# A planner's prices for VectorE and GpSimd working side by side, ten staging tiles, and two early steps for two batches

## The chip, the cores and the metric

The kernel runs on one core of a Trainium2 chip. The metric is the device time in microseconds (us) of one execution. A profiled execution gives the span from its first to its last instruction, a trace of every instruction on each engine, and the TensorE clock that was granted.

The engines are named as in the profile: PE is TensorE (matrix products), PEld its weight loads, DVE is VectorE, ACT is ScalarE, POOL is GpSimd, SP is SyncE, which issues nearly all DMAs. Each engine executes its own queue strictly in order and waits on semaphores for the others.

## The reference

Chunked attention with a few memory keys, then a gated feed-forward layer whose gate mixes positions:

```python
# q, k, v: 4 batches, 8 heads, 768 positions, 64 wide; mem_k, mem_v: 8 rows
for c in range(24):                       # chunks of 32 queries
    k_full = concat(mem_k, k[c*32-16 : c*32+40]); v_full = likewise
    a = softmax(q_c @ k_full.T / 8)
    out_c = a @ v_full
x = out as (4, 768, 512)
h = relu(x @ w_in)                        # 512 x 1024
u, v = h[..., :512], h[..., 512:]
v_n = (v - mean(v)) / sqrt(var(v) + 1e-6) # over the last axis
v_s = w_spatial @ v_n + b_spatial         # 768 x 768 over positions
y = (u * v_s) @ w_out                     # 512 x 512
```

All arrays are float32.

## The kernel before

**Arithmetic.** The feed-forward and later products split each fp32 operand into a high part (a cast on ScalarE) and a low part (a subtraction of the cast from the original, on VectorE or GpSimd), and use three matmuls: high x high, low x high, high x low. The spatial product and the product with w_out are each done by a scheme of seven half-size products, p1 to p7, in place of eight. Sums and differences of left operands (`total`, L651) and their two parts (`left`, cast L664 and subtraction L667) are made on the fly; those of right operands are made once from w_spatial and w_out (`right_hand`, L881, and `split`, L853 and L857).

**Stages.** (1) 24 attention units, each four chunks of one batch for all heads: scores and the previous unit's weighted values in one burst of matmuls (L395), maximum, subtraction, exponent, sum (`softmax`), a transpose (L475), the scaling of the result (L430), a transpose back (L490) and its split into high and low (L495, L499). (2) The feed-forward products `ffn_v` and `ffn_u` (L528 to L530) are interleaved with attention and run on to the end of that stage. ffn_v's result is normalised in a staging tile and stored to DRAM; ffn_u's is stored directly. (3) For each batch, `spatial(b)`: steps p1, p2, p6, p5, p7, p4, p3. Each step has two output tiles of 128 x 384, nine matmuls each. The results are copied out of PSUM into staging tiles (ACT L731), joined with other banks (DVE L737) and multiplied into u on GpSimd (L745, the gate). (4) For each batch, `ffn_o(b)`: steps p1, p6, p5, p7, p4, p3, p2 on the gated tiles, with copies (L780), joins (L786) and stores.

w_in and w_out arrive as the two 32-bit halves of float64 numbers. `from_f64` unpacks a row block: two ScalarE scalings (L824, L829), two VectorE operations (L833 and L834, called the shift) and a GpSimd addition (L839). w_out can be put in place only when the feed-forward products are done, since its tiles take the memory of w_in.

**Buffers.** `sizes` gives the tiles of each ring. `st` is the staging ring, 8 tiles of 128 x 512: ffn_v results, unpacked weight rows, temporaries of `right_hand` for w_out, and results of (3) and (4) before they are joined or gated. A tile is given again when the use eight allocations back has ended. PSUM rings: `f` has 3 banks, `y` 5. The gated tiles `ug` are 6, the normalised halves `vr` 2.

**The plan.** The kernel first only records operations, each with an engine, a price in us, what it reads and writes, and a rank. `Plan.order` then simulates the engines by these prices: at each turn it takes, over all engines, the operation that can start earliest, and among several of one engine that could start at the same time the one of lowest rank. The order of planned starts is the order of each engine's queue. An operation marked `alone` (the shift, and ffn_v's normalisation) is planned only where GpSimd is free, and GpSimd waits for its planned end. Prices are linear in the width:

```python
    def act(n): return 0.18 + 0.00087 * n
    def dve(n): return 0.17 + 0.00102 * n
    def pool_(n): return 0.15 + 0.0024 * n
```

Neither a VectorE operation nor a GpSimd one is priced differently where the other engine works at the same time.

Ranks: attention unit i has 10 i; ffn products on PE 10000 plus a running number `seq`; unpacking and splitting w_out 260; totals, left operands, copies, joins and gates of (3) and (4) 1000 + `seq`; matmuls of (3) and (4) 10000 + `seq`. `seq` grows in the order in which the steps are defined, so the loop at L1004 sets who comes first: for each batch b it defines the loads, then step p1 of `spatial(b)` (L1012), then `ffn_o(b - 1)`, then the other steps of `spatial(b)`. For b = 3 one step of `ffn_o(2)`, its last, is held back until after the first of `ffn_o(3)`.

Of the kernel before, what the change touches and what calls it, by code (L numbers as in the profile page):

```python
# [25 lines left out]
class Plan:  # L26
# [12 lines left out]

    def op(self, eng, us, fn, r=(), w=(), rank=0.0, mb=0.0, tail=0.0, after=None, alone=False, drag=1.0):  # L40
        n = len(self.ops)
        deps, begun = set(), set()
        if after is not None:
            begun.add(after)
        for key in r:
            deps.add(self.writer.get(key))
            self.readers.setdefault(key, []).append(n)
        for key in w:
            deps.add(self.writer.get(key))
            deps.update(self.readers.get(key, ()))  # L50
            self.writer[key], self.readers[key] = n, []
        deps -= {None, n}
        held = {k[:2] for k in (*r, *w) if isinstance(k, tuple) and k[0] in self.rings}
        for s in held:
            if s not in self.slots and s[0] not in self.loose:
                if s[0] in self.newest:
                    begun.add(self.newest[s[0]])
                self.newest[s[0]] = n
            self.slots.setdefault(s, []).append(n)
        begun -= deps  # L60
        self.ops.append((eng, us, fn, deps, rank, mb, tail, held, begun, alone, drag))
        return n

    def order(self):
# [8 lines left out]
        pipe, landed = self.landing, []  # L73
        lone = 0.0
        taken = {ring: [] for ring in self.rings}
# [6 lines left out]
        while len(out) < len(ops):  # L82
# [20 lines left out]
            (t, _, n), e = best  # L103
            _, us, _, _, _, mb, tail, held, _, alone, drag = ops[n]
            for s in held:
# [4 lines left out]
            if alone:  # L110
                lone = t + us
            if mb:
                pipe = max(pipe, t + us) + mb * drag / self.rate
                end[n] = pipe + self.landing
                landed.append((end[n], mb))
            else:
                end[n] = t + us + tail
# [25 lines left out]
def tile_chunked_attention_gmlp(  # L143
# [43 lines left out]

    sizes = {"f": 3, "sx": 1, "pt": 2, "xt": 1, "y": 5, "st": 8, "big": 4, "uo": 2, "x": 2, "vm": 3,
             "q": 2, "k": 2, "kT": 2, "p": 1, "xs": 1, "pT": 1, "vr": 2, "op": 4, "sm": 2, "ug": 6, "ot": 11}
# [6 lines left out]
    def dve(n):  # L196
        return 0.17 + 0.00102 * n
# [194 lines left out]
    def burst(i, rank, split=False):  # L392
# [19 lines left out]
        for what in (whole if split else [whole]):  # L412
            reads, writes = [], []
            us = 0.4
            if "s" in what:
                reads += qk_keys(i, "q") + [("kmain", i % NK, 0), ("kmain", i % NK, 1), ("kmem", i % NK)]
                writes.append(("sx", i, 0))
                us += 0.6
            if "a" in what:
                reads += [("pT", i - 1)] + v_keys(i - 1)  # L420
                writes.append(("sx", i, 1))
                us += 0.7
            op("PE", us, lambda what=what: go(what), r=reads, w=writes, rank=rank, tail=0.25)
# [11 lines left out]
    def softmax(i, rank):  # L435
# [30 lines left out]
        op("ACT", act(512), exp, w=[("p", i)], rank=rank)  # L466
        op("DVE", dve(512) + 0.36, den, r=[("p", i)], w=[("rec", i)], rank=rank + 0.6)

    def flip(i, rank):
        if i < NU:  # L470
# [6 lines left out]
            def copy():  # L477
                nc.scalar.copy(alloc("pT", i, [P, T, P], F32), t_["pt", i])
            op("PE", 0.45, turn, r=[("p", i)], w=[("pt", i)], rank=rank, tail=0.25)
            op("ACT", act(512) - 0.04, copy, r=[("pt", i)], w=[("pT", i)], rank=rank)  # L480
        if i >= 1:
# [15 lines left out]
            def low():  # L497
                x = t_["x", n]
                nc.vector.tensor_tensor(x[:, 1, :, o:o + UT], t_["xt", j], x[:, 0, :, o:o + UT].bitcast(F32),  # L499
                                        op=ALU.subtract)  # L500
            op("PE", 0.45, turn_x, r=[("xs", j)], w=[("xt", j)], rank=rank - 0.5, tail=0.25)
            op("ACT", act(512) - 0.04, high, r=[("xt", j)], w=[("x", n, tt, "h")], rank=rank - 0.5)
# [46 lines left out]
    def ffn_v(b, tt):  # L549
# [31 lines left out]
        op("ACT", act(512), relu, r=[("f", n)], w=[k_], rank=rank)  # L581
        op("DVE", 1.05, stat, r=[k_], w=[("ve", i)], rank=rank)
        op("POOL", 0.6, power, r=[("ve", i)], w=[("rstd", i)], rank=rank)
# [53 lines left out]
    def product(kind, b, steps, halves, chunks, width, parts, N, right, right_keys, sum_eng, seed, done):  # L637
# [5 lines left out]
        def total(name, in0, in1, o, keys, to=None):  # L643
# [3 lines left out]
            def go():  # L647
# [3 lines left out]
                {"DVE": nc.vector, "POOL": nc.gpsimd}[sum_eng].tensor_tensor(a, in0(), in1(), op=o)  # L651
            op(sum_eng, dve(W) if sum_eng == "DVE" else pool_(W), go, r=keys, w=[sm], rank=rank)
            return (lambda: t_[sm].rearrange("p (s n) -> p s n", s=chunks)), [sm]

        def left(name, of, keys):
# [12 lines left out]
            op("ACT", act(W), high, r=keys, w=[(*ok, "h")], rank=rank)  # L668
            op("DVE", dve(W), low, r=[*keys, (*ok, "h")], w=[(*ok, "l")], rank=rank)
            return half, [(*ok, "h"), (*ok, "l")]  # L670
# [178 lines left out]
    def split(eng, n, dst, of, reads, writes, rank):  # L849
# [8 lines left out]
        op("ACT", act(n), high, r=reads, w=[(*w, "h") for w in writes], rank=rank)  # L858
        op(eng, pool_(n) if eng == "POOL" else dve(n), low, r=[*reads, *[(*w, "h") for w in writes]], w=writes, rank=rank)

# [143 lines left out]
    for b in range(B + 1):  # L1004
        if b < B:
# [5 lines left out]
            spatials.append(spatial(b))  # L1011
            next(spatials[b])  # L1012
        if b:
# [59 lines left out]
```

## Time and profile before

| | us |
|---|---|
| median of 3 runs (lowest, highest) | 395.51 (395.07, 395.77) |
| the profiled execution, its own time | 395.85 |
| its span, first to last instruction | 394.1 |
| PE busy in the span | 368.4 (93%) |
| DVE busy | 281.0 (71%) |
| ACT busy | 210.2 (53%) |
| POOL busy | 157.5 (40%) |

The granted TensorE clock was 1.000 throughout. Shares are averages over stages with different limits. In a timeline row, the columns are the start and the duration in us, the engine, the line of the program, the operation with what it writes and reads, and a count where several are merged; a bracket gives the idle time of that engine directly before the row and the instruction whose end ended it. Waits are read from semaphores, so where one instruction waits for several, the last of them is named. In the chain of waits, a piece's length is the part of it that lies on the chain.

### The profile page before, as it was taken

To read this page: it belongs to the slowest core of one execution; us is meant where nothing else is said; L and a number is where in the kernel's file an instruction comes from. 1 tells how busy PE (TensorE), PEld (TensorE's weight loads), DVE (VectorE), ACT (ScalarE), POOL (GpSimd) and SP (SyncE) were. 2 spreads that over 40 slices of the span, in tenths; PEclk is the share of its full clock that TensorE was granted. 3 is DMA by queue.
4 is the path that set the end of the run, shared out by engine and by line. 5 is a ranking of instruction groups with operands and counts; after the bars stand their busy time and mean duration, and the time that the engine had idled before them with its cause. 6 is when DMAs were issued, how large, how long until landed. Compare 5 with 4: busy or idle time off the path is not lost.

```text
span 394.1 us, 8707 instructions
## 1 busy us (share of the span) xinstructions
PE 368.4 (93%) x3428; PEld 335.0 (85%) x3428; DVE 281.0 (71%) x465; ACT 210.2 (53%) x368; POOL 157.5 (40%) x161
## 2 busy tenths in 40 slices
PE   1659899999999999999999998899999999999996
PEld 1437688898898988988889898799999999999996
DVE  7975965756856558866575499978956794788594
ACT  4765646575456557464434475438434734473361
POOL 8433762193621177601012968770226033403520
PEclk9999999999999999999999999999999999999999
DMA  8998567676575683786603768403640562040014
GB/s 231 309 232 210 129 202 230 183 251 185 182 219 160 235 221 112 211 223 206 187 29 136 257 237 278 136 25 121 210 153 0 162 233 89 0 175 27 2 40 161
DMA packets 47356, 64.93 MB, mean 165 GB/s; under 512 B 4434, under 2 KB 38866, under 8 KB 47316
## 3 DMA queue, kind: packets, MB, share of 16 engines
q1 hardware_dynamic: 46900, 64.25, 53.5%
q8 instruction: 27, 0.44, 0.5%
q10 hardware_dynamic: 416, 0.13, 0.1%
q14 instruction: 13, 0.11, 0.1%
HBM read 45.49 MB, written 18.87 MB: 163 GB/s over the span
## 4 chain that ended last, share of the span: by engine, by line
PE 80%; DVE 8%; issue 2%; ACT 2%; POOL 1%; ACTq 0%
PE y L689 16%; PE f L689 12%; PE f L528 12%; PE sx L395 11%; PE f L530 11%; PE f L529 11%; PE xt L490 3%; PE pt L475 3%; DVE wout L857 2%; DVE sm L651 2%; DVE op L667 2%; POOL ug L745 1%; DVE st L737 1%; ACT op L664 1%; DVE st L834 0%
## 5 line engine op out<-in xcount | busy, mean ns | idle before, releaser
L745 POOL TENSOR_TENSOR ug<-st,ug 128x384 f32<-128x384 f32 x32 | 43.8, 1380 | 79.6 <-DVE st L737 62.0
L528 PE MATMUL f<-x,win_h 128*128 128x384 f32 x128 | 45.8, 358 | 0.0
L574 POOL TENSOR_TENSOR rstd<-ve,mhalf 128x1 f32<-128x1 f32 x24 | 13.5, 562 | 77.4 <-DVE ve L570 75.7
L664 ACT CAST op<-sm 128x768 fp32r<-128x768 f32 x32 | 26.3, 837 | 32.5 <-DVE sm L651 29.9
L530 PE MATMUL f<-x,win_h 128*128 128x384 f32 x128 | 43.2, 338 | 0.0
L529 PE MATMUL f<-x,win_l 128*128 128x384 f32 x128 | 43.0, 336 | 0.0
L528 PE MATMUL f<-win_h,x 128*128 128x512 f32 x96 | 41.6, 433 | 0.0
L689 PE MATMUL y<-wsp,op 128*128 128x384 f32 x192 | 39.5, 341 | 2.0 <-ACT st L731 1.2
L395 PE MATMUL sx<-kmain,q 128*32 128x128 f32 x768 | 28.5, 294 | 11.3 <-ACT kmain L377 9.3
L377 ACT COPY kmain<-k 64x640 f32<-64x640 f32 x48 | 34.7, 724 | 6.8 <-DMA k<-in_k_dram 4.0
L530 PE MATMUL f<-win_l,x 128*128 128x512 f32 x96 | 38.2, 398 | 0.0
L529 PE MATMUL f<-win_h,x 128*128 128x512 f32 x96 | 38.1, 397 | 0.0
L430 DVE TENSOR_TENSOR xs<-sx,rec 128x512 f32<-128x512 f32 x24 | 16.6, 690 | 29.7 <-PE sx L395 29.7
L667 DVE TENSOR_TENSOR op<-sm,op 128x768 fp32r<-128x768 f32 x32 | 33.6, 1056 | 5.3 <-ACT op L664 4.9
L689 PE MATMUL y<-wout,op 128*128 128x256 f32 x288 | 36.2, 280 | 0.8 <-ACT ot L780 0.7
L395 PEld LDWEIGHTS sx<-kmain,q 128*32 128x32 f32 x768 | 21.5, 117 | 18.2 <-POOL vmain L369 10.1
L689 PEld LDWEIGHTS y<-wsp,op 128*128 128x128 f32 x192 | 33.9, 188 | 3.2 <-ACT st L731 1.9
L689 PEld LDWEIGHTS y<-wout,op 128*128 128x128 f32 x288 | 34.9, 188 | 1.2 <-ACT ot L780 0.9
L369 POOL COPY vmain<-memv 8x1024 f32<-8x1024 f32 x22 | 23.8, 1083 | 17.6 <-PE sx L395 16.2
L689 PE MATMUL f<-wsp,op 128*128 128x384 f32 x144 | 29.4, 339 | 1.5 <-DVE op L667 1.5
L599 ACT ACTIVATE uo<-f 128x384 f32<-128x384 f32 x32 | 15.6, 490 | 26.8 <-PE f L530 17.7
L689 PE MATMUL f<-wout,op 128*128 128x256 f32 x216 | 27.3, 280 | 0.0
(100 smaller groups left out, 833.4 us busy)
## 6 DMA issues: line engine op xcount, KB each, us to landing
vmain<-in_v_dram SPq DMA_DIRECT2D x48, 128.0 KB
vn_far<-st SPq DMA_DIRECT2D x24, 256.0 KB
u_far<-uo SPq DMA_DIRECT2D x32, 192.0 KB
vr<-vn_far SPq DMA_DIRECT2D x8, 768.0 KB
ug<-u_far SPq DMA_DIRECT2D x16, 384.0 KB
q<-in_q_dram SPq DMA_DIRECT2D x11, 512.0 KB
out_dram<-ot SPq DMA_DIRECT2D x36, 128.0 KB
vmain<-in_v_dram SPq DMA_DIRECT2D x47, 96.0 KB
```

The lines of the kernel that those rows point to most:

```text
L369: {"DVE": nc.vector, "POOL": nc.gpsimd}[eng].tensor_copy(to, of)
L377: nc.scalar.copy(kmain[i % NK][rows, :, r, :, 0:CH], k_of(i)[rows].rearrange("p t (c s) -> p t c s", s=CH))
L395: nc.tensor.matmul(o, w_, m, start=True, stop=True, skip_group_check=True)
L430: nc.vector.tensor_tensor(xs, t_["sx", i][:, 1], rec.unsqueeze(3).broadcast_to([P, T, 2, D]), op=ALU.mult)
L528: nc.tensor.matmul(o, lh, rh, start=(j == 0), stop=False)
L529: nc.tensor.matmul(o, ll, rh, start=False, stop=False)
L530: nc.tensor.matmul(o, lh, rl, start=False, stop=(j == len(pairs) - 1))
L599: op("ACT", act(HT), lambda: nc.scalar.activation(alloc("uo", i, [P, HT], F32), t_["f", n], AF.Relu), r=[("f", n)], w=[("uo", i)], rank=rank)
L664: nc.scalar.copy(half(0), of())
L667: nc.vector.tensor_tensor(half(1), of(), half(0).bitcast(F32), op=ALU.subtract)
L689: nc.tensor.matmul(o, x, y, start=first and m == 1 and not (seed and bank != "x"), stop=m == 3 * chunks, skip_group_check=True)
L745: nc.gpsimd.tensor_tensor(g, t_[st(x)], g, op=ALU.mult)
```

## The change

1. `op` takes a mark `shared`. In `order`, when a marked VectorE operation is placed at a time when GpSimd's planned work is not over, its price grows by (1 - 1/1.75) of the overlap left, at most by 0.75 of the price. When any GpSimd operation is placed while the last marked VectorE operation is not over, its price grows likewise with 1.4 in place of 1.75. Marked are `den` in `softmax`, the statistics of `ffn_v`, `total`, the subtraction in `left` (L667), and the subtraction in `split` where VectorE does it (L857).
2. Prices: a burst with both scores and values 1.70 to 1.88, one with values alone 1.10 to 1.00; `den` by 0.07 more; a transpose 0.45 to 0.47; the statistics 1.05 to 1.08.
3. The ring `st` has 10 tiles in place of 8.
4. At L1012, batches 1 and 2 define two steps of `spatial(b)` (p1 and p2) ahead of `ffn_o(b - 1)`; batches 0 and 3 one, as before.

```diff
-    def op(self, eng, us, fn, r=(), w=(), rank=0.0, mb=0.0, tail=0.0, after=None, alone=False, drag=1.0):
+    def op(self, eng, us, fn, r=(), w=(), rank=0.0, mb=0.0, tail=0.0, after=None, alone=False, drag=1.0, shared=False):
...
-        lone = 0.0
+        lone = both = 0.0
...
-            _, us, _, _, _, mb, tail, held, _, alone, drag = ops[n]
+            _, us, _, _, _, mb, tail, held, _, alone, drag, shared = ops[n]
+            beside, pace = {"DVE": (free["POOL"] if shared else 0.0, 1.75), "POOL": (both, 1.4)}.get(e, (0.0, 1.0))
+            if beside > t:
+                us += min((beside - t) * (1 - 1 / pace), us * (pace - 1))
...
+            if shared:
+                both = t + us
...
-    sizes = {"f": 3, "sx": 1, "pt": 2, "xt": 1, "y": 5, "st": 8, "big": 4, "uo": 2, "x": 2, "vm": 3,
+    sizes = {"f": 3, "sx": 1, "pt": 2, "xt": 1, "y": 5, "st": 10, "big": 4, "uo": 2, "x": 2, "vm": 3,
...
-                us += 0.7
+                us += 0.88 if "s" in what else 0.6
...
-        op("DVE", dve(512) + 0.36, den, r=[("p", i)], w=[("rec", i)], rank=rank + 0.6)
+        op("DVE", dve(512) + 0.43, den, r=[("p", i)], w=[("rec", i)], rank=rank + 0.6, shared=True)
...
-            op("PE", 0.45, turn, r=[("p", i)], w=[("pt", i)], rank=rank, tail=0.25)
+            op("PE", 0.47, turn, r=[("p", i)], w=[("pt", i)], rank=rank, tail=0.25)
...
-        op("DVE", 1.05, stat, r=[k_], w=[("ve", i)], rank=rank)
+        op("DVE", 1.08, stat, r=[k_], w=[("ve", i)], rank=rank, shared=True)
...
-            op("DVE", dve(W), low, r=[*keys, (*ok, "h")], w=[(*ok, "l")], rank=rank)
+            op("DVE", dve(W), low, r=[*keys, (*ok, "h")], w=[(*ok, "l")], rank=rank, shared=True)
...
-            next(spatials[b])
+            for _ in range((1, 2, 2, 1)[b]):
+                next(spatials[b])
```

`total` and `split` get the mark in the same way as `left`, where their engine is VectorE, and the transpose back gets the price of the transpose.

More of the change, by code (lines that the diff above doesn't have):

```diff
@@ L60, in op @@
         begun -= deps
-        self.ops.append((eng, us, fn, deps, rank, mb, tail, held, begun, alone, drag))
+        self.ops.append((eng, us, fn, deps, rank, mb, tail, held, begun, alone, drag, shared))
         return n
@@ L500, in low @@
                                         op=ALU.subtract)
-            op("PE", 0.45, turn_x, r=[("xs", j)], w=[("xt", j)], rank=rank - 0.5, tail=0.25)
+            op("PE", 0.47, turn_x, r=[("xs", j)], w=[("xt", j)], rank=rank - 0.5, tail=0.25)
             op("ACT", act(512) - 0.04, high, r=[("xt", j)], w=[("x", n, tt, "h")], rank=rank - 0.5)
@@ L651, in go @@
                 {"DVE": nc.vector, "POOL": nc.gpsimd}[sum_eng].tensor_tensor(a, in0(), in1(), op=o)
-            op(sum_eng, dve(W) if sum_eng == "DVE" else pool_(W), go, r=keys, w=[sm], rank=rank)
+            op(sum_eng, dve(W) if sum_eng == "DVE" else pool_(W), go, r=keys, w=[sm], rank=rank,
+               shared=sum_eng == "DVE")
             return (lambda: t_[sm].rearrange("p (s n) -> p s n", s=chunks)), [sm]
@@ L858, in split @@
         op("ACT", act(n), high, r=reads, w=[(*w, "h") for w in writes], rank=rank)
-        op(eng, pool_(n) if eng == "POOL" else dve(n), low, r=[*reads, *[(*w, "h") for w in writes]], w=writes, rank=rank)
+        op(eng, pool_(n) if eng == "POOL" else dve(n), low, r=[*reads, *[(*w, "h") for w in writes]], w=writes, rank=rank,
+           shared=eng == "DVE")
     def w_in_part(c, part, rank, load_rank, sub_eng):
```

## The prediction

> **What bounds the kernel now.** I read three views in this order: busy time by stretch, the timelines of TensorE, ScalarE (ACT), VectorE (DVE) and GpSimd (POOL) where TensorE has gaps, and the chain of waits. The stretches are cut where the work changes: start, attention with the first products, the change-over to the spatial product, the steady middle and the end.
>
> ```profile
> 0.00:60.00 60.00, 41.77 (x472) 31.80 (x473) 45.98 (x81) 35.34 (x60) 32.83 (x42) 1.00 0.82 220
> 60.00:233.60 173.60, 173.60 (x1931) 152.43 (x1930) 112.02 (x227) 95.95 (x163) 65.88 (x76) 1.00 0.63 191
> 233.60:268.30 34.70, 30.60 (x174) 28.86 (x172) 31.38 (x33) 17.90 (x34) 26.15 (x19) 1.00 0.43 147
> 268.30:360.00 91.70, 91.70 (x637) 91.70 (x638) 70.60 (x96) 47.39 (x88) 25.00 (x18) 1.00 0.37 126
> 360.00:394.10 34.10, 30.68 (x221) 30.16 (x219) 21.07 (x31) 13.60 (x27) 7.68 (x7) 1.00 0.17 59
> sum 394.10, PE 368.36 PEld 334.95 DVE 281.04 ACT 210.18 POOL 157.54; mean PE 73.67 PEld 66.99 DVE 56.21 ACT 42.04 POOL 31.51
> ```
>
> Columns are the stretch, its length, then busy us and instructions of PE, PE's weight load, DVE, ACT and POOL. TensorE (PE) does 368.36 us of work that the change neither adds to nor takes from. Its gaps are 60.00 - 41.77 = 18.23 us at the start, none to 233.6, 34.70 - 30.60 = 4.10 at the change-over, none to 360, and 34.10 - 30.68 = 3.42 at the end: 25.75 together. Two stretches that hold 265 of 394 us have no gap at all, so an order of work that is better there for VectorE or GpSimd brings nothing. The change can shorten only the 18.23 and the 4.10; it can lengthen anything. The change-over's gaps, one by one:
>
> ```profile
> 246.07 1.15 PE L689 MATMUL f<-wsp,op 128*128 128x384 f32 x5 [1.47 <-DVE op L667]
> ...
> 250.68 1.14 PE L689 MATMUL y<-wsp,op 128*128 128x384 f32 x5 [0.62 <-DVE op L667]
> ...
> 254.31 1.31 PE L689 MATMUL y<-wsp,op 128*128 128x384 f32 x6 [0.38 <-ACT st L731]
> ...
> 256.99 1.32 PE L689 MATMUL y<-wsp,op 128*128 128x384 f32 x6 [0.84 <-ACT st L731]
> ...
> 268.25 2.37 PE L689 MATMUL y<-wout,op 128*128 128x256 f32 x18 [0.67 <-ACT ot L780]
> ```
>
> The number in brackets is the gap before the row, and what ended it. 1.47 + 0.62 come from a VectorE subtraction (L667, the low half of a left operand), 0.38 + 0.84 from a copy out of PSUM on ScalarE (L731), 0.67 from another such copy (L780). That is 3.98 of the 4.10; the 0.12 left is spread too thin to treat. Each engine runs its queue in the order that the plan wrote, so I look at what stands ahead of those releasers. ScalarE first:
>
> ```profile
> 253.26 0.62 ACT L853 CAST wout<-st 128x512 fp32r<-128x512 f32 x1 [0.75 <-POOL st L881]
> 253.78 0.47 ACT L731 COPY st<-y 128x384 f32<-128x384 f32 x1
> 255.94 0.62 ACT L853 CAST wout<-st 128x512 fp32r<-128x512 f32 x1 [1.68 <-POOL st L881]
> 256.46 0.86 ACT L731 COPY st<-y 128x384 f32<-128x384 f32 x2
> ```
>
> Before both copies (253.78 and 256.46, L731) stands a cast of w_out (L853) that itself waited 0.75 and 1.68 us for GpSimd. The copies' banks were done: ScalarE was held by an instruction that was queued too early. VectorE:
>
> ```profile
> 242.73 1.61 DVE L857 TENSOR_TENSOR wout<-st,wout 128x512 fp32r<-128x512 f32 x1
> 244.26 0.55 DVE L737 TENSOR_TENSOR st<-f,st 128x384 f32<-128x384 f32 x1
> 244.73 1.29 DVE L667 TENSOR_TENSOR op<-sm,op 128x768 fp32r<-128x768 f32 x1
> ...
> 249.68 0.95 DVE L667 TENSOR_TENSOR op<-sm,op 128x768 fp32r<-128x768 f32 x1
> 250.54 2.07 DVE L667 TENSOR_TENSOR op<-vr,op 128x768 fp32r<-128x768 f32 x1
> ...
> 260.98 0.96 DVE L667 TENSOR_TENSOR op<-ug,op 128x768 fp32r<-128x768 f32 x1 [1.78 <-ACT op L664]
> ```
>
> The subtraction that PE waits for at 246.07 (244.73, L667) stands behind a subtraction for w_out (242.73, 1.61) and a join (244.26, L737). No bracket stands in the first five rows: VectorE has work without a break, 31.38 of 34.70 us in this stretch. The last row shows the first pause, 1.78 us, after 258. So two different faults make the change-over's gaps: a queue in the wrong order (ScalarE) and a full engine (VectorE).
>
> **The change, part by part.** No instruction is added or removed. What changes is what the plan believes, and so the order in each queue and the slot that a tile takes.
>
> *VectorE and GpSimd stretch each other.* The plan gets prices that grow when marked VectorE operations run beside GpSimd work. In the trace they do grow:
>
> ```profile
> 249.89 1.90 POOL L839 TENSOR_TENSOR big<-st,big 128x512 uint32<-128x512 uint32 x1 [2.01 <-ACT op L664]
> ```
>
> Here GpSimd's w_out addition (L839) runs 249.89 to 251.79 and VectorE's L667 of 250.54 takes 2.07 instead of the 0.95 of the row before it, 1.12 more. The old plan charges 0.95 there. By the new formula the overlap left at that start is 251.79 - 250.54 = 1.25 us, so it adds at most 1.25 x (1 - 1/1.75) = 0.54: the plan comes half way to the trace.
>
> What that brings at ScalarE: a plan that sees GpSimd's w_out steps end later puts the two L853 casts behind the copies. Gain 0.38 + 0.84 = 1.22 if both move, 0 if neither does. I take 1.22, since the casts' own waits (0.75 and 1.68) are each longer than the gap that they caused, so even half of the correction should reverse the pair. What is late next is VectorE's join at 256.37 and GpSimd's gates, which PE does not wait for until the product with w_out. The casts, then later by the length of a copy, feed subtractions for w_out that are needed from 265 on.
>
> What it brings at VectorE: the w_out subtractions carry rank 260 and the spatial product's carry 1000 and more, so when both are ready w_out goes first, under either plan. More honest prices make VectorE look fuller, and do not change that rule. The waits of 1.47 and 0.62 may go (-2.09) when w_out operands look ready later, or two more w_out subtractions may come ahead of operands that PE waits for. Their price:
>
> ```profile
> L857 DVE TENSOR_TENSOR wout<-st,wout 128x512 fp32r<-128x512 f32 x4 | 4.8, 1189 | 0.0
> ```
>
> 2 x 1.19 = +2.38. The row shows 1189 ns as the mean. Between -2.09 and +2.38 I take 0, nearest to what a full engine gives: total VectorE work is the same.
>
> The Trainium skill, "SBUF — State Buffer", "Who interferes with whom", says that of a VectorE instruction with two SBUF inputs and a GpSimd instruction that reads SBUF, the later one is blocked until the other ends; nothing is shared by rate. The rows above agree: held to 251.79 and then 0.95 would end at 252.74, and 250.54 + 2.07 is 252.61. By that rule the new plan still misplaces by 0.6 us each time, the order is no nearer to the chip's, and the ScalarE gain would be 0 in place of 1.22; this is the first rival below.
>
> *Two early steps for batches 1 and 2.* The spatial step p2 of batch 1 moves ahead of the w_out product of batch 0 (L1012). Its duration, and that of a whole attention burst, from the chain of waits:
>
> ```profile
> 70.20 1.88 PE sx L395 x64
> ...
> 297.27 3.17 PE f L689 x18
> ```
>
> A p2 step is 18 matmuls, 3.17 us. PE waits 0.67 at 268.25, in the first step of the w_out product; with 3.17 us of ready matmuls ahead, that copy (L780) has been done for 3.17 - 0.67 = 2.5 us when PE comes. With the 1.22 from above PE comes earlier by that much, and 1.3 are left. Gain 0.67. What moves along: one ScalarE cast (ScalarE is busy 17.90 of 34.70), one VectorE subtraction (0.95) and two joins (2 x 0.55), then two GpSimd gates (26.15 of 34.70 busy). VectorE's 0.95 + 1.10 = 2.05 us rank behind batch 0's spatial steps and before the w_out product's sums; the pause of 1.78 takes most, and the sums come 0.3 us later while PE has 3.17 more to do. No transfer moves: the gated tiles and both halves of batch 1 are loaded in either order, so SP's queue is passed by nothing. If the cover fails (the subtraction lands before 258, where VectorE is full), its 0.95 falls on PE: range -0.67 to +0.95, and I take -0.67, as the ranks place it behind. Batch 2: no gap in 268.3 to 360, so 0; its cover is PE's own work there, 91.70 of 91.70 us, and if an operand came late one subtraction, 0.95, would show.
>
> *Ten staging tiles.* Nothing executes for this. Following the ring of eight in order of allocation, the second staging copy of batch 1 takes the tile that batch 0's last gate frees; that wait lies inside the 0.67 already counted. Elsewhere the tile wanted had been free. 0 beyond that; with more freedom the w_out rows might be unpacked earlier, a part of the -2.09.
>
> *PE prices* (burst 1.70 to 1.88, as the row of 1.88 has it; transposes 0.45 to 0.47; an attended half alone 1.10 to 1.00). 18 x 0.18 + 48 x 0.02 - 6 x 0.10 = 3.6 us more plan time for attention. PE has no gap from 60 to 233.6, and attention precedes the feed-forward by rank in any case: 0; without that cover one late operand costs what PE paid at the start.
>
> *The start.* It has the most idle time, and the plan now stretches its four w_in subtractions:
>
> ```profile
> 22.00 0.69 DVE L857 TENSOR_TENSOR win_l<-st,win_h 128x512 fp32r<-128x512 f32 x1 [0.42 <-ACT win_h L853]
> 22.60 0.42 DVE L833 TENSOR_SCALAR st<-st 128x512 uint32<-128x512 uint32 x1
> 23.06 0.69 DVE L834 SCALAR_TENSOR_TENSOR st<-big,st 128x512 uint32<-128x512 uint32 x1
> 23.67 0.68 DVE L430 TENSOR_TENSOR xs<-sx,rec 128x512 f32<-128x512 f32 x1
> ```
>
> ```profile
> 24.41 1.11 PE L490 MATMUL xt<-ident,xs 128*128 128x128 f32 x4 [2.87 <-DVE xs L430]
> 27.10 1.94 PE L395 MATMUL sx<-kmain,q 128*32 128x128 f32 x32 [1.58 <-ACT kmain L377]
> ```
>
> PE waited 2.87 us for the scaling L430 at 23.67, which stands behind a subtraction (0.69) and a shift (0.42 + 0.69). Were those behind it, PE would go on 1.8 us sooner; were a second such trio ahead, 1.8 later. The new prices can do either: -1.8 to +1.8, and I take 0 for want of a row nearer to one end. The end of the kernel keeps one early step for batch 3: 0.
>
> **Sum.** -1.22 - 0.67 = -1.89. The profiled execution took 395.85 (span 394.1 and 1.75 around it), 0.34 over the median of 395.51. From the median: 395.51 - 1.89 = 393.6.
>
> **Rivals.** About 0.2%, 0.8 us, is what a measurement of this kernel can tell from no change.
> 1. *The prices change but the order does not where it counts*: the casts stay ahead of the copies, and only the early step pays, 395.51 - 0.67 = 394.8, within 0.2%. For it: the correction is half of what the trace shows. Against: the casts' waits are longer than the gaps. The skill's rule above speaks for this one.
> 2. *VectorE turns worse, and it ends slower*: two more w_out subtractions ahead of the operands of the steps at 246 and 250. The joins behind them keep ScalarE's gain from showing: 395.51 - 0.67 + 2.38 = 397.2. It decides from 0.8 + 0.67 = 1.47 us, more than one subtraction of 1.19. For it: rank 260 before 1000, VectorE without a break. Against: priced longer, w_out operands also look ready later.
> 3. *More falls than I count*: the VectorE waits go as well, 393.6 - 2.1 = 391.5. For it: 1.47 has only one 1.61 us subtraction ahead of it that is not needed before 265. Against: the engine stays full.
> 4. *The start slips by a trio*: 393.6 + 1.8 = 395.4, no change to be seen. For it: the gaps there hang on one order of four operations. Against: nothing marks that trio more than others.
>
> **Numbers.** Forecast 0.37, rival 3 0.18, rival 1 0.14, rival 4 0.07, rival 2 0.24. Faster 0.37 + 0.18 = 0.55, same 0.21, slower 0.24. The forecast alone would span 392.8 to 394.6. The range takes in rivals 3 and 2 and part of the start's 1.8: 391.5 - 1.0 = 390.5, and 397.2 + 0.6 = 397.8; beyond lie cases with both the start and VectorE moving one way, some 0.2.
>
> **What would show it.** Right: between 233 and 270 PE's gaps come to about 2.2 us, no L853 cast with a wait on GpSimd right before an L731 copy, 36 spatial matmuls (p1 and p2 of batch 1) directly before the first w_out matmul, and no gap in it. Rival 1: the rows at 254 and 257 keep their brackets. Rival 2: two or more w_out rows in a run before an L667, with brackets over 2 us on PE. Rivals 3 and 4 are read from the gaps of the first 60 us and from the L667 brackets. Wrong altogether if PE shows gaps between 60 and 233 or between 270 and 360, or if its busy time changes from 368.

## The result, and the profile after

The changed kernel is slower by 0.8%: 398.66 us (median of 4 runs, 398.27 to 399.33) against 395.29 (4 runs of the kernel before beside them, 394.66 to 395.77), a ratio of 1.0083 with an interval of 1.0065 to 1.0102. The forecast was 393.6, the range ended at 397.8. The profiled execution took 399.02, with a span of 397.2 us (394.1 before). First the busy time by stretch, with the columns as before; the third stretch is longer, since the change-over now ends later.

```profile
0.00:60.00 60.00, 42.57 (x471) 32.38 (x472) 46.59 (x79) 35.22 (x59) 32.72 (x42) 0.97 0.83 221
60.00:233.60 173.60, 173.60 (x1934) 152.47 (x1932) 109.77 (x229) 95.24 (x163) 65.67 (x76) 1.00 0.62 186
233.60:275.00 41.40, 35.10 (x194) 33.80 (x193) 37.12 (x39) 20.56 (x37) 31.14 (x23) 0.96 0.42 143
275.00:360.00 85.00, 85.00 (x600) 85.00 (x599) 64.75 (x88) 43.73 (x83) 18.49 (x15) 1.00 0.41 136
360.00:397.20 37.20, 33.79 (x238) 33.31 (x236) 23.72 (x34) 15.48 (x29) 10.37 (x8) 1.00 0.16 54
```

TensorE has no gap from 60 to 233.6 and none from 275 to 360, as before. Its gaps are 17.43 us at the start (18.23 before), 41.40 - 35.10 = 6.30 at the change-over (4.10) and 3.41 at the end (3.42). Together they grow by 1.39 us. But the span grew by 3.1, and TensorE's busy time, 370.06 for the same matmuls, holds the other 1.70: some matmuls ran slower. The column of the granted clock says where, 0.97 at the start and 0.96 at the change-over, where the kernel before has 1.00. For the start the two can't be compared: the clock's record begins at 29.1 us in this execution and at 32.6 in that of the kernel before, and what lies ahead of it counts as full clock. There, under the 1.00, bursts of 32 attention matmuls took 1.94 us in both kernels, and 1.08 right behind it. At the change-over both have a record. TensorE at the change-over:

```profile
234.09 0.34 PE L689 MATMUL y<-bias,ones 128*128 128x384 f32 x1
...
252.46 1.15 PE L695 MATMUL y<-wsp,op 128*128 128x384 f32 x5 [1.56 <-DVE op L673]
253.44 0.68 PE L695 MATMUL y<-wsp_end,op 128*128 128x384 f32 x3
253.96 1.22 PE L695 MATMUL y<-wsp,op 128*128 128x384 f32 x6
...
260.26 1.14 PE L695 MATMUL y<-wsp,op 128*128 128x384 f32 x5 [0.74 <-DVE op L673]
...
267.84 1.81 PE L695 MATMUL f<-wsp,op 128*128 128x384 f32 x5 [4.00 <-DVE op L673]
269.45 1.17 PE L695 MATMUL f<-wsp_end,op 128*128 128x384 f32 x3
270.41 1.70 PE L695 MATMUL f<-wsp,op 128*128 128x384 f32 x6
```

The spatial product begins at 234.09 (234.26 before) and from there to the end it is 397.2 - 234.09 = 163.11 us, against 394.1 - 234.26 = 159.84: the whole loss, 3.27, lies behind this point. In place of the four gaps of batch 0's spatial product that the prediction listed (1.47, 0.62, 0.38, 0.84: 3.31) there are now two, 1.56 in its step p4 and 0.74 in batch 1's p1: 1.01 better. The 0.67 in the product with w_out has gone. In its place stands a gap of 4.00 us at 267.84, inside the step p2 of batch 1 that the change moved ahead. And the 14 matmuls behind it took 271.94 - 267.84 = 4.10 us, where the same 5, 3 and 6 at 252.46 took 255.03 - 252.46 = 2.57: another 1.53. So -1.01 - 0.67 + 4.00 + 1.53 = 3.85, of which 3.27 show at the end; 0.12 of the rest are pauses of before too small to list, and 0.46 I did not trace. What VectorE had in its queue:

```profile
249.86 1.68 DVE L840 SCALAR_TENSOR_TENSOR st<-big,st 128x512 uint32<-128x512 uint32 x1
251.46 0.94 DVE L673 TENSOR_TENSOR op<-vr,op 128x768 fp32r<-128x768 f32 x1
...
263.51 1.74 DVE L656 TENSOR_TENSOR sm<-ug 128x768 f32<-128x768 f32 x1 [1.42 <-POOL ug L751]
265.29 1.63 DVE L656 TENSOR_TENSOR sm<-sm,ug 128x768 f32<-128x768 f32 x1
266.84 0.94 DVE L673 TENSOR_TENSOR op<-vr,op 128x768 fp32r<-128x768 f32 x1
```

The step waits for the subtraction of 266.84 (L673). Its cast had been ready since 263.2 (ScalarE, L670, at 262.33 for 0.84). Ahead of it on VectorE stand two sums for the product with w_out (L656), 1.74 and 1.63 us, and the first of them had waited 1.42 us for GpSimd's gates. The first gap of 1.56 has the same form: a subtraction at 251.46 behind the shifts of w_out (L839, L840).

Why the gates are late is followed in the timeline from the end of attention on: VectorE's last split of attention's result (L499, now L504), the loads of w_out on the sync engine's queue (SPq), GpSimd's last splits of w_spatial and its run of gates; first the kernel before, then after.

```profile
214.87 0.69 DVE L499 TENSOR_TENSOR x<-xt,x 128x512 fp32r<-128x512 f32 x1 [2.07 <-ACT x L495]
...
221.02 6.03 SPq L256 DMA_DIRECT2D big<-in_moe_w_out_dram  x3
223.01 5.01 POOL L857 TENSOR_TENSOR wsp_end<-big,wsp_end 128x768 fp32r<-128x768 f32 x2
232.76 0.40 SPq L256 DMA_DIRECT2D big<-in_moe_w_out_dram  x1
...
257.00 6.80 POOL L745 TENSOR_TENSOR ug<-st,ug 128x384 f32<-128x384 f32 x5 [1.09 <-DVE st L737]
```

```profile
216.79 0.69 DVE L504 TENSOR_TENSOR x<-xt,x 128x512 fp32r<-128x512 f32 x1 [2.09 <-ACT x L500]
...
223.87 0.33 SPq L261 DMA_DIRECT2D big<-in_moe_w_out_dram  x1
230.12 3.87 POOL L863 TENSOR_TENSOR wsp_end<-big,wsp_end 128x768 fp32r<-128x768 f32 x1 [0.81 <-ACT wsp_end L859]
239.61 0.33 SPq L261 DMA_DIRECT2D big<-in_moe_w_out_dram  x1
...
259.35 6.75 POOL L751 TENSOR_TENSOR ug<-st,ug 128x384 f32<-128x384 f32 x5
```

Attention ends 1.9 us later (214.87 to 216.79), though the spatial product starts at the same time: in the order of TensorE's queue there are 93 matmuls of the feed-forward product left behind the last attended half, where there were 105. The last split of w_spatial goes from 228.0 to 234.0, the fourth load of w_out from 232.8 to 239.6, and GpSimd's run of five gates from 257.0 to 259.4.

### The profile page after: what moved, and what is told of

It is laid out like the page before. It is cut to its first block, busy times and chain, and to the rows that moved or that the text cites. A ratio compares the mean times of both kernels' runs of the same rounds, so it can differ in the third digit from the quotient of the medians.

```text
span 397.2 us, 8690 instructions
## 1 busy us (share of the span) xinstructions
PE 370.1 (93%) x3428; PEld 337.0 (85%) x3428; DVE 281.9 (71%) x465; ACT 210.2 (53%) x368; POOL 158.4 (40%) x161
## 4 chain that ended last, share of the span: by engine, by line
PE 80%; DVE 7%; DMA 6%; ACT 3%; issue 3%; POOL 1%; SPq 0%; ACTq 0%
PE y L695 17%; PE f L695 13%; PE f L533 12%; PE sx L400 11%; PE f L534 11%; PE f L535 11%; PE xt L495 3%; PE pt L480 2%; DMA vmain<-in_v_dram 2%; DMA u_far<-uo 1%; DMA k<-in_k_dram 1%; DMA ug<-u_far 1%; DVE sm L656 1%; DVE st L840 1%; DVE op L673 1%
## 5 line engine op out<-in xcount | busy, mean ns | idle before, releaser
L751 POOL TENSOR_TENSOR ug<-st,ug 128x384 f32<-128x384 f32 x32 | 42.8, 1350 | 81.5 <-DVE st L743 48.2
L579 POOL TENSOR_TENSOR rstd<-ve,mhalf 128x1 f32<-128x1 f32 x24 | 14.6, 606 | 68.5 <-DVE ve L575 68.1
L435 DVE TENSOR_TENSOR xs<-sx,rec 128x512 f32<-128x512 f32 x24 | 16.5, 689 | 32.9 <-PE sx L400 32.9
L673 DVE TENSOR_TENSOR op<-sm,op 128x768 fp32r<-128x768 f32 x32 | 33.2, 1039 | 3.6 <-ACT op L670 3.2
L695 PE MATMUL f<-wsp,op 128*128 128x384 f32 x144 | 30.7, 350 | 4.0 <-DVE op L673 4.0
L737 ACT COPY st<-y 128x384 f32<-128x384 f32 x32 | 15.3, 478 | 32.1 <-PE y L695 30.7
L670 ACT CAST op<-sm 128x768 fp32r<-128x768 f32 x32 | 26.1, 836 | 8.3 <-DVE sm L656 6.9
L695 PEld LDWEIGHTS f<-wsp,op 128*128 128x128 f32 x144 | 26.5, 196 | 4.5 <-DVE op L673 4.3
```

What stands on the lines that cost most here:

```text
L435: nc.vector.tensor_tensor(xs, t_["sx", i][:, 1], rec.unsqueeze(3).broadcast_to([P, T, 2, D]), op=ALU.mult)
L670: nc.scalar.copy(half(0), of())
L673: nc.vector.tensor_tensor(half(1), of(), half(0).bitcast(F32), op=ALU.subtract)
L695: nc.tensor.matmul(o, x, y, start=first and m == 1 and not (seed and bank != "x"), stop=m == 3 * chunks, skip_group_check=True)
L737: op("ACT", act(HT), lambda: nc.scalar.copy(alloc("st", st(x)[1], [P, HT], F32), t_[bank]), r=[bank], w=[st(x)], rank=rank)
L751: nc.gpsimd.tensor_tensor(g, t_[st(x)], g, op=ALU.mult)
```

## The experiments

Each was timed in rounds against the kernel before on the same chip. In the table, "tail" is the time from the first matmul of the spatial product to the end in the profiled execution (159.84 before, 163.11 after), which leaves out the start; "gaps" are TensorE's of 0.3 us and more from 236 to 300. A profile is one execution: a7's took 399.54 and e1's 401.84, each at an end of its kernel's spread. "After" is the changed kernel.

| kernel | median us | ratio (interval) | tail | gaps |
|---|---|---|---|---|
| b1: before + early steps | 396.06 | 1.0016 (1.0006 to 1.0026) | 160.65 | 1.48 .62 .39 .84 1.29 |
| b2: before + ten tiles | 395.69 | 1.0005 (.9996 to 1.0014) | 159.93 | 1.49 .62 .39 .82 .72 |
| c2: before + burst prices | 399.80 | 1.0112 (1.0088 to 1.0136) | 163.55 | 2.52 1.66 .61 |
| c4: before + stretch | 398.76 | 1.0074 (1.0058 to 1.0091) | 163.87 | 1.56 .89 3.28 .41 |
| b3: before + prices, stretch | 399.24 | 1.0095 (1.0081 to 1.0109) | 163.92 | 1.56 .91 3.26 .41 |
| a1: after, one step | 399.98 | 1.0117 (1.0104 to 1.0130) | 163.81 | 1.55 .73 2.86 .41 |
| a2: after, batch 2 one step | 399.24 | 1.0098 (1.0079 to 1.0117) | 163.07 | 1.55 .75 3.99 |
| a7: after, no stretch | 402.71 | 1.0160 (1.0132 to 1.0188) | 162.12 | 2.54 1.06 .66 |
| e1: before, attention late | 400.01 | 1.0099 (1.0072 to 1.0127) | 165.23 | 2.55 1.19 1.55 .61 |
| e2: after, rank 20 | 398.20 | 1.0057 (1.0037 to 1.0077) | 162.82 | 1.19 .74 3.99 |
| e4: before, rank 20 | 395.92 | 1.0007 (.9998 to 1.0016) | 160.00 | 1.69 .62 .35 .84 .70 |
| a3: after, sums told | 395.78 | 1.0005 (.9991 to 1.0020) | 160.44 | 1.58 .73 .51 1.09 |
| b4: b1, sums told | 395.81 | 1.0006 (.9997 to 1.0016) | 160.20 | 1.47 .62 .38 .84 .41 .36 |
| e3: a3, rank 20 | 395.28 | .9994 (.9979 to 1.0010) | 159.96 | 1.18 .72 .49 1.08 |
| a4: after, 12 fillers | 398.76 | 1.0076 (1.0053 to 1.0099) | 163.04 | 1.56 .74 1.94 |
| a9: after, 24 fillers | 396.85 | 1.0026 (1.0010 to 1.0043) | 161.52 | 1.57 .73 |
| f1: e3, 5 fillers at start | 394.16 | .9969 (.9958 to .9980) | 159.95 | 1.19 .74 .50 1.08 |
| f2: f1, 7 more fillers | 393.24 | .9942 (.9929 to .9954) | 159.91 | 1.19 .74 .52 1.07 |

### Which part costs

The edits of a1, a2 and b1 are the tuple of steps, those of b2 the ring, of a7 `if False:` in place of `if beside > t:`. c4 is the kernel before with the stretch alone, b3 with the stretch and all prices, and c2 has the smallest edit of all:

```diff
-                us += 0.7
+                us += 0.88 if "s" in what else 0.6
```

**a1, one step for every batch.** 

> The changed kernel with one early step for every batch, as before. Theory A (the early step of batch 1 meets a VectorE queue in which its operand's subtraction stands behind two sums): the PE gap of 4.00 us and the slow matmuls behind it, 1.6 us, go, and at most the 0.67 us wait of the kernel before comes back: 393.1 to 393.8 us. Theory B (the new prices spoil VectorE's order in the change-over, whatever PE takes first): a similar wait stands before the product with w_out, 397 us or more.

**a2, two steps for batch 1 alone.** 

> The changed kernel with two early steps for batch 1 alone. Theory A: batch 2 has no gap to lose, so as the changed kernel, about 398.7 us. If batch 2's second step were to blame, about 393.5 us. Theory B: 398.7 us too.

**a7, no stretch.** 

> The changed kernel with its new prices, ten tiles and early steps, but the stretch formula off. Theory C (the stretch makes GpSimd look late to the plan, which moves the last w_spatial splits and the unpacking of w_out about 6 us later, so GpSimd's gates start 2.3 us later and all that waits for them with it): w_out loads come back to 221 to 233 us, the gap of 4 us goes, 394 to 395.5 us. Theory D (the ten tiles or the corrected burst prices move the order): 398 us or more.

**b1, the early steps alone.** 

> The kernel before with two early steps for batches 1 and 2 and nothing else. As predicted for this part: the 0.67 us wait goes, 394.7 us. If VectorE's queue puts the two sums ahead of the early step's subtraction here too: PE waits 2 us or more, 397 us.

**b2, ten tiles alone.** 

> The kernel before with ten staging tiles and nothing else. Theory C: no change, 395.4 us (395.0 to 395.8). Theory D: 397 us or more, with w_out's loads late.

**b3, prices and stretch.** 

> The kernel before with the new prices and the stretch, eight tiles and one early step. Theory C: all of the harm is here, 398.5 to 400 us, w_out's loads from 224 to 240 us. Theory D with the tiles as the cause: 395 us; with the corrected prices as the cause: as under C, and then the run without the stretch tells them apart.

**c2, the burst's price alone.** 

> The kernel before with the corrected burst prices (1.88 and 1.00) and nothing else; 93 matmuls are left after attention here too. Theory E: 397.5 to 400 us, without any stretch. Theory F: 395.4 us (prices alone are harmless).

**c4, the stretch alone.** 

> The kernel before with the stretch formula and nothing else; 93 matmuls are left after attention. Theory E: 397.5 to 400 us. If only the corrected burst prices harm: 394 to 395.5 us, with the ScalarE copies no longer late.

Ten tiles and batch 2's second step do nothing, as forecast. The early steps alone cost 0.16%: the 0.67 goes, a wait of 1.29 on the moved step's subtraction comes. The loss comes with either repricing, each by itself: the burst's price 1.1%, the stretch 0.7%. Taking away a part of the change does not help either (a1, a7). In a7 w_out's loads come at 225.4, 230.9, 239.7 and 240.8, no sooner than with the stretch, so it isn't the stretch that makes them late. In c2, c4 and b3, as in the changed kernel, 93 matmuls stand behind the end of attention. What replaces the old gaps differs: TensorE waits at a copy out of PSUM without the stretch (c2, first fence), at a cast of the w_out product's left operand with it (a1, second fence).

```profile
254.81 2.29 PE L689 MATMUL y<-wsp,op 128*128 128x384 f32 x6 [2.52 <-ACT st L731]
...
271.67 3.80 PE L689 MATMUL y<-wout,op 128*128 128x256 f32 x17 [0.61 <-DVE op L667]
```

```profile
268.92 0.58 PE L695 MATMUL y<-wout,op 128*128 128x256 f32 x1 [2.86 <-ACT op L670]
269.91 4.00 PE L695 MATMUL y<-wout,op 128*128 128x256 f32 x17 [0.41 <-DVE op L673]
```

In both, the matmuls behind are slow: 6 in 2.29 us (1.22 is usual), 17 in 3.80 and 4.00 (18 take 2.27). So the two early steps are where the 4.00 shows, and not the reason for it: with one step (a1) the wait moves to the product with w_out.

### Is it the late end of attention?

The theory (E, where an expectation gives it that letter): the prices cost nothing in attention, but they put one feed-forward group ahead of its end, and that makes w_out late. e1 does this alone, with the old prices, by making the last transpose of an attended half wait in the plan for one more group:

```diff
+            turned[j] = op("PE", 0.45, turn_x, r=[("xs", j)], w=[("xt", j)], rank=rank - 0.5, tail=0.25)
...
+            if (n, j) == (48, 0):
+                plan.ops[turned[NU - 1]][3].add(m)
```

> The kernel before; only the last transpose of attention on PE is planned behind one more feed-forward group, so that 93 matmuls (18.1 us) of feed-forward are left after attention, as in the changed kernel, in place of 105 (20.2 us). Theory E (the last w_spatial splits, which need attention's memory, and behind them w_out's loads and unpacking start 2.1 us later, and the change-over has no room for it): 397.5 to 399 us, w_out's loads late. Theory F (the harm is in how the new prices order the change-over itself): 395.2 to 396 us.

It costs 1.0%, with nothing repriced: the late end is enough for a loss of this size. Its gaps are of c2's kind, 2.55 and 1.19 at ScalarE's copies, and not those of the changed kernel. e2 and e4 then bring forward what it delays: `w_sp_pair(HU - 1, 20.0)` for 205.0, the rank of the last pair of w_spatial's row blocks.

> The changed kernel with the last w_spatial pair at rank 20 in place of 205, so that its splits on GpSimd go ahead of ffn_v's small powers. Theory E: the last split ends about 2 us sooner, so do w_out's loads: 396.5 to 398 us. Theory F: 398.7 us.

> The kernel before with the last pair of w_spatial at rank 20 and nothing else. If when the last split ends sets the w_out loads and through them the change-over, this kernel's 4.1 us of gaps there shrink by 0.5 to 1.5 and the ratio is 0.997 to 0.999. If its gaps come from the order of VectorE's queue alone, 1.000 within 0.001; a new order that brings the waits on ScalarE of the run with a late attention gives 1.003 and more.

In e2 the loads of w_out come at 222.54, two from 229.47 on, and at 237.26 (223.87, 228.98, 234.02 and 239.61 in the changed kernel), so the last comes 2.3 us sooner, and the gap of 3.99 stays. The time, 398.20, lies between the two theories and is not clear of the changed kernel's. The kernel before gains nothing (e4). So a link of my chain is weak: the loads are late, but that does not make the 4.00.

### Is it the order of VectorE's queue?

a3 leaves everything late and only tells the plan that the first sum for a w_out product comes after the next batch's subtraction for the moved step:

```diff
-            op(sum_eng, ..., go, r=keys, w=[sm], rank=rank,
+            op(sum_eng, ..., go, r=[*keys, *([("low", "s", b + 1, "a12")] if kind == "o" and b < 2 and name == "s1" else [])], w=[sm], rank=rank,
...
-            op("DVE", dve(W), low, r=[*keys, (*ok, "h")], w=[(*ok, "l")], rank=rank, shared=True)
+            op("DVE", dve(W), low, r=[*keys, (*ok, "h")], w=[(*ok, "l"), ("low", *tag, name)], rank=rank, shared=True)
```

> The changed kernel with all its early steps; only the plan is told that the first sum of the w_out product comes after the subtraction for step p2 of the next batch. Theory A: the 4.00 us gap and the 1.6 us of slow matmuls go, 393.1 to 394 us. Theory B: no gain, 398 us or more. If the early step hurts by what else it moves (casts, joins), something between, 396 us.

VectorE's timeline in a3:

```profile
262.80 1.09 DVE L673 TENSOR_TENSOR op<-vr,op 128x768 fp32r<-128x768 f32 x1 [1.11 <-ACT op L670]
263.81 1.75 DVE L656 TENSOR_TENSOR sm<-ug 128x768 f32<-128x768 f32 x1
```

On VectorE the subtraction now comes 262.80 - 233.66 = 29.1 us after the start of the spatial product, where it took 266.84 - 234.09 = 32.8, and the sum behind it (L656) no longer waits for the gates. The gap of 4.00 becomes 0.51, the slow matmuls go, and 2.9 us come back: 395.78, level with the kernel before although attention still ends late.

**b4, the same in b1.** 

> The kernel before with the two early steps, its own prices, and the order told: the first sum of a w_out product comes after the next batch's subtraction for the moved step. With the early steps alone TensorE lost the 0.67 before w_out but paid 1.29 for a subtraction, 396.06. If the two sums ahead of that subtraction are what it waited for, the 1.29 goes and the time is 0.67 under the kernel before, a ratio of about 0.998. Rival: the sums, now later, hold the w_out product instead, 0.5 us and more, and the ratio is 1.000 or above.

The 1.29 and the 0.67 both go, but 0.41 and 0.36 come, and the ratio is 1.0006: there the rival was right. The two early steps are worth nothing at their best.

**e3, a3 with rank 20.** 

> The changed kernel with the sums after the subtraction (which alone gave 395.78) and the last pair of w_spatial at rank 20. If the late last split still costs there by way of the w_out loads, the remaining gaps at the change-over (1.58, 0.73, 0.51, 0.27, 1.09) shrink by 0.7 to 1.5 us in all and the time is 394.5 to 395.2, under the kernel before. If lateness costs only through the sums, it is 395.6 to 396.0; the wait of 1.19 on ScalarE's copy that the rank alone brought may come back and make it 396.5.

Level with the kernel before, and the interval also holds a3's value: that the rank helps is not shown. What is shown, then: a late end of attention costs 1% by itself under the old order (e1), and in the changed kernel two sums ahead of one subtraction hold nearly all of the loss (a3). By which of the late operations the end of attention reaches the 4.00 stays open, since sooner loads did not change it (e2). How the 4.00 comes about can be read against b1, which has the same early steps and 1.29. Counted from the start of the spatial product, TensorE stops for the operand at 29.75 us (263.84) and not at 31.34, and goes on at 33.75 and not at 32.63: of the 2.71 more, 1.59 are TensorE's coming sooner and 1.12 VectorE's being later.

### Why are matmuls slow behind a gap?

a4 puts overwritten matmuls into the gap of 4.00, at the head of batch 1's p2; a9 puts in 24. The result is overwritten by the step that follows.

```diff
+                    for _ in range(12 if tag == ("s", 1) and bank == "x" and n[-1] == 0 else 0):
+                        nc.tensor.matmul(o, ones, bias[:, 0], start=True, stop=True, skip_group_check=True)
```

> The changed kernel with 12 matmuls of 128x384 whose result is overwritten, issued on PE at the head of step p2 of batch 1, into its own bank, so that PE is idle for about 1.9 in place of 4.0 us. If PE slows because it stood idle for 4 us: the matmuls behind the gap run at full rate, 1.6 us less, about 397.1 us, granted clock nearer 1. If the slowing has another cause (what runs beside, the kind of matmul): 398.7 us. If filling costs PE itself time: above 398.7 us.

> The changed kernel with 24 matmuls of ones by the bias, overwritten by the step that follows, at the head of batch 1's second spatial step (12 in the earlier run, which cut TensorE's gap from 4.00 to 1.94 us and did not move the time). If the matmuls behind the gap are slow because TensorE stood idle before them, a gap cut to 0.3 us or less leaves them at their usual 1.14, 0.68 and 1.22 us for rows of 5, 3 and 6, and the time is 398.7 - 1.6 = 397.1. If they are slow for another reason (the operand arrives late again and again, or what runs beside them), they stay at 1.5 to 1.8, 1.1 and 1.7 to 2.0 us and the time stays at 398.5 to 398.9.

TensorE's rows, a4 and then a9:

```profile
268.54 1.46 PE L697 MATMUL f<-wsp,op 128*128 128x384 f32 x5 [1.94 <-DVE op L673]
269.80 1.16 PE L697 MATMUL f<-wsp_end,op 128*128 128x384 f32 x3
270.76 2.04 PE L697 MATMUL f<-wsp,op 128*128 128x384 f32 x6
```

```profile
261.31 4.33 PE L689 MATMUL f<-bias,ones 128*128 128x384 f32 x24
265.48 1.33 PE L697 MATMUL f<-wsp,op 128*128 128x384 f32 x6
266.64 0.68 PE L697 MATMUL f<-wsp_end,op 128*128 128x384 f32 x3
```

With 12 the gap is 1.94 and the matmuls behind it are as slow as behind 4.00. With 24 there is no gap; 3 matmuls take 0.68 and not 1.17, the granted clock from 240 on is 1.00, and the tail falls by 1.59, the 1.53 of above. VectorE's subtraction comes no sooner (264.66 - 231.88 = 32.8 us behind the start of the spatial product, as without fillers), so it is TensorE's standing idle that made the matmuls slow. The granted clock (third column from the end) around the 4.00 of the changed kernel:

```profile
264.64:268.05 3.41, 0.21 (x1) 0.21 (x2) 3.38 (x4) 1.31 (x3) 1.46 (x1) 1.00 0.00 0
268.05:271.46 3.41, 3.41 (x12) 3.41 (x12) 2.28 (x4) 0.52 (x1) 0.17 (x1) 0.50 0.00 0
271.46:274.87 3.41, 3.41 (x28) 3.41 (x27) 2.81 (x4) 1.17 (x3) 3.05 (x2) 1.00 0.00 0
```

The Trainium skill, "TensorE: Matmul & The Clock Gate", "What's actually happening", says that an idle window of about 3.4 us halves the clock until a busy window of that length has passed, and that the window is free-running. The length of the slow spell agrees (0.50 for 3.41 us, behind the gap of 4.00); the idle time doesn't: 1.94 us were enough.

The clock records of the 20 traces show how much was enough. In each of them the clock changes only at points that lie a multiple of 3.41 us apart, and these points lie differently in each execution. They divide TensorE's time into fixed windows. The clock was halved behind each of the 41 windows at full clock in which TensorE stood idle for 1.9 us or more in all, behind one of the five with 1.69 to 1.82, and behind none of the 1326 with less. So what counts is the idle time inside one window, in one gap or in two, and not the length of a gap. c2's gap of 2.52 lies almost whole in one window (2.47), and the matmuls behind it are slow at once. a7's gap of 2.54 ends 1.3 us before its window does (252.63 to 256.04, 2.13 idle): the six matmuls right behind it still take 1.31, and the clock is halved from 256.04 on.

The start shows the same. In the changed kernel and in a9 it has the same order; the profiled executions, the changed kernel first:

```profile
40.77 0.66 PE L480 MATMUL pt<-ident,p 128*128 128x128 f32 x4 [1.36 <-ACT p L458]
42.44 0.53 PE L534 MATMUL f<-win_h,x 128*128 128x512 f32 x1 [0.79 <-DVE x L504]
43.32 1.94 PE L400 MATMUL sx<-vmain,pT 128*32 128x128 f32 x32
```

```profile
40.08 0.65 PE L480 MATMUL pt<-ident,p 128*128 128x128 f32 x4 [1.33 <-ACT p L458]
41.76 0.50 PE L534 MATMUL f<-win_h,x 128*128 128x512 f32 x1 [0.79 <-DVE x L504]
42.42 1.08 PE L400 MATMUL sx<-vmain,pT 128*32 128x128 f32 x32
```

The same pair of gaps, and behind it 32 matmuls in 1.94 us in one execution and in 1.08 in the other. In the changed kernel the window from 39.36 to 42.77 holds 2.15 us of idle time, and the clock is 0.50 in the next one; in a9 the border of two windows divides the pair, 1.75 in the window from 37.97 to 41.39 and 0.37 in the next, and the clock stays at 1.00. The window runs freely, as the same section of the Trainium skill has it, and these two traces agree. a9's 12 times fall in two groups, 5 from 395.11 to 395.27 and 7 from 396.77 to 397.95; its profile is of the first. The five have a mean granted clock of 0.995, the seven of 0.985 to 0.994: that fits, but only one of the twelve has a trace. f1 fills the 1.34 of this pair in e3, f2 also the 3.40 before 24.6 us:

```diff
                 a = alloc("pt", i, [P, T, P], F32, psum=True)
+                for _ in range(5 if i == 3 else 0):
+                    nc.tensor.matmul(a.rearrange("p t w -> p (t w)"), win_h[:, 0, DH:DH + P], win_h[:, 0, DH:], start=True, stop=True, skip_group_check=True)
...
             a = alloc("xt", j, [P, T, P], F32, psum=True)
+                for _ in range(7 if j == 0 else 0):
+                    nc.tensor.matmul(...)
```

> The changed kernel with the sums after the subtraction and the last w_spatial pair at rank 20 (395.28 alone), and five overwritten matmuls of 128x512 in the gap of 1.34 us before the fourth transpose of the probabilities at the start. If the pair of gaps there (1.34 and 0.78) is what makes some executions slow (the matmuls behind it at 1.9 in place of 1.08 us in one profile, not in another), the slow executions go: the upper times at 395 to 396.5 disappear and the median is 393.4 to 394.5, a ratio under 0.998, below both kernels. If the slow spells at the start have another cause, the times stay spread over 393.4 to 396.5 with a median of 395.0 to 395.5.

> As the other of this pair, and seven more overwritten matmuls in the gap of 3.4 us before the first transpose of an attended half (24.6 us). Behind that gap the matmuls of 24.6 to 30 us ran at 0.63 us in place of 0.40 and 1.94 in place of 1.08. If it is TensorE's idle time that makes them slow, they run at their full rate and the time falls by 1 to 2.5 us more, to 391.5 to 393.5, unless VectorE or ScalarE, which these matmuls feed, are no sooner ready: then 0 to 0.5. If not idle time, no change, or 0.5 us worse where the seven matmuls outlast the gap.

```profile
25.33 1.94 PE L400 MATMUL sx<-kmain,q 128*32 128x128 f32 x32
```

```profile
21.24 2.57 PE L497 MATMUL xt<-win_h 128*128 128x512 f32 x7
25.05 1.08 PE L400 MATMUL sx<-kmain,q 128*32 128x128 f32 x32
```

The row above is f1's, the two below it f2's. With the seven fillers (21.24) the burst behind them takes 1.08 us and not 1.94, and f2's five times lie within 0.17 us (393.16 to 393.33), where e3's spread over 3.1 (393.38 to 396.50). f1's median is where it was expected, with one of its ten times, 395.25, still among the upper ones; f2's is 0.92 lower, just short of the 1 us. f1 gains 0.31% and f2 0.58% against the kernel before: f2 beats both kernels. Its tail is 159.91, no better than before's 159.84; all of the gain is at the start. It speaks for the fillers and not for the change: no run has them in the kernel before.

## Why the prediction was wrong

- **The failed step: the PE prices.** It said "PE has no gap from 60 to 233.6, and attention precedes the feed-forward by rank in any case: 0". c2 shows 1.12% for the burst's price alone. A price needs no gap in its own stage: it moves one feed-forward group from behind the last attended half to ahead of it, and the cost comes some 40 us later. The stretch, which the prediction counted at -1.22, moves the same group and costs 0.74% by itself (c4). The step's own condition ("without that cover one late operand costs what PE paid at the start") was looked for in the wrong stage.
- **The second failed step: the early step's cover.** It said that the moved VectorE work ranks "behind batch 0's spatial steps and before the w_out product's sums", and that its 0.95 falls on TensorE if that fails. In the queue two sums came first, and what falls on TensorE is not the instruction's own 0.95 but all that stands ahead of it, the wait for the gates too: 4.00. Rank decides only among operations that could start together, so by the plan's prices the sum must have been able to start sooner. The predicted sign, 36 spatial matmuls before w_out with no gap in them, did not come.
- **A missing term.** No step asked what a long gap does to the matmuls behind it: 1.53 us here. It turned the loss from 1.7 into 3.3.
- **ScalarE's 1.22: the size was near, the reason was not shown.** The two rows are gone in every kernel with the stretch but e2, e3, f1 and f2, where one of 1.18 to 1.19 is back; without it, c2, a7 and e1 have 2.5. But the casts did not go behind the copies, as ScalarE's timeline in the changed kernel shows:

```profile
257.29 0.62 ACT L859 CAST wout<-st 128x512 fp32r<-128x512 f32 x1 [2.65 <-POOL st L888]
257.82 0.47 ACT L737 COPY st<-y 128x384 f32<-128x384 f32 x1
```

A cast that waited 2.65 us for GpSimd stands right before a copy (others, with waits of 1.36 and 1.78, before the copies at 251.35 and 254.17), the very sign that was to be absent. TensorE does not pay here, and the order of the rows shows why. Step p4 goes on in the banks of p7, so it waits for p7's two copies. In the kernel before these are the ones at 253.78 and 256.46. In the changed kernel the waits of 1.47 ahead of p7 and of 0.62 in it are gone, and TensorE is through with p7 16.5 us after the start of the spatial product and not after 19.7. Its copies, at 249.18 and 251.35, end 0.9 and 2.1 us before p4's first matmul in each bank (250.56 and 253.96). The copies at 254.17 and 257.82 are p4's own, and TensorE does not wait for them.

- **VectorE's "Between -2.09 and +2.38 I take 0"**: 1.56 is left of the 2.09 in batch 0 and 0.74 comes in batch 1's p1, 2.30 in all: near. The price lay in batch 1's p2.
- **Ten tiles 0, batch 2 0**: right (b2 1.0005; a2 has the same gaps as the changed kernel).
- **The start 0**: -0.17 in the profile, but by chance: the plan did let TensorE go on earlier (25.47 for the burst at 27.10), and a slow spell took it back. In a9's profile the spatial product begins at 231.88, 2.4 earlier than before.
- **The rivals.** The second had the right sign and engine. Its place was batch 0's spatial product and its price two w_out subtractions, 2.38; the runs show the sums, in batch 1's p2. The first had its mechanism half right, since the casts did stay ahead of the copies; but the brackets on ScalarE, which it would have kept, went.

## What to carry to other kernels

A corrected price in a planner that takes what is ready first can reorder work that has no slack, far from the place that was repriced: compare the order of the queues at the next change of stage before trusting that a full stage hides it. When an operation is moved ahead, price its operand by everything that stands ahead of it in its engine's queue, waits included, or tell the planner the order. A TensorE gap of 2 us cost nearly twice its length here (1.94 and 1.5 behind it, a4). Overwritten matmuls paid for themselves where they filled it (a9) and did nothing where they left 1.94 us (a4).

## What the hardware did that I had not expected

Matmuls ran at about half rate behind gaps of 1.94, 2.52, 2.86 and 4.00 us, and behind a pair of 1.66 and 0.61; not behind single gaps of 1.56 to 1.58 (after, a3) or 1.69 (e4). Behind gaps of 2.54 (a7) and 2.55 (e1) they ran at full rate for 1.3 to 1.4 us first. Behind a pair of 1.33 to 1.36 and 0.79 the same order did so in one execution and not in another. A gap can be cut in half and cost the same (a4). What decides in all of these is the idle time that falls into one window of 3.41 us, and where the windows lie changes from execution to execution: 1.9 us and more halved the clock each time, less than 1.69 never did.
